# Infini-attention beside a gated MLP on one core: value projection of chunk 0 first, x copied by VectorE alone, first weights split over both load queues

## Chip, core and metric

One core of one Trainium2 chip. The metric is the device time of one execution in microseconds (us). Before the change it was 273.81 us (median of three runs, 273.72 to 274.2).

## The reference, cut to what matters

```python
def reference(A_x, A_wq, A_wk, A_wv, A_wo, A_beta, B_x, B_W_gate, B_W_up, B_W_down, gate_w):
    x = A_x                                   # [1, 2048, 512] bf16
    g = sigmoid((x * gate_w).sum(-1, keepdims=True))
    a = _A_ref(x, A_wq, A_wk, A_wv, A_wo, A_beta)     # 32 heads of 16, 4 segments of 512 tokens:
                                              # q, k, v = x @ wq, x @ wk, x @ wv; causal softmax within a
                                              # segment, mixed with a memory M, z carried over segments; @ wo
    b = _B_ref(x, B_W_gate, B_W_up, B_W_down) # relu(x @ W_gate) * (x @ W_up) @ W_down
    return g * a + (1 - g) * b
```

Segment (chunk) 0 has no memory yet. Its q, k and v projections are the first real work of the kernel.

## The kernel before

The kernel builds a list of operations for each engine. A list scheduler of its own then places them with a cost model and emits every engine's program in the order so found. A small change at the start can therefore change the order of everything that follows.

```python
    x0 = A_x[0, 0:512, :].rearrange("(i p) d -> p i d", p=128)
    for i, eng in enumerate(("sp", "act", "sp", "act")):
        load(eng, [f"hT{i}"], V.hT[:, i, :], x0[:, i, :], 1 << 17)
    for nm, w, src in (("wq", V.wq, A_wq), ("wk", V.wk, A_wk), ("wv", V.wv, A_wv)):
        for kt in range(KT):
            load("act" if nm == "wq" and kt % 2 else "sp", [f"{nm}{kt}"], w[:, kt, :], ...)
    # ... (cut)
    xps, xcs = [warm(5, 0, 3)], []            # 5 dummy matmuls on a zeroed tile
    for i in range(4):                        # transpose x: 4 matmuls against the identity per token tile
        # ... (cut) fx
        xps.append(pe(fx, 430, reads=[f"hT{i}", "ident"], writes=[f"bankL{i}"], name=f"xt{i}"))
        if i % 2 == 0:                        # PSUM -> xT, by turns on VectorE and ScalarE
            xcs.append(dve(... tensor_copy ..., name=f"xc{i}"))
        else:
            xcs.append(act(... activation Copy ..., name=f"xc{i}"))
    xps.append(warm(4, 1, 0))                 # 4 more dummies
    # ... (cut) inside proj(s): q and k tiles stream all 512 tokens of xT,
    #     v tiles use 128 tokens of xT as weights and stream wv
        if s == 0:
            pes = [p for k in "qkv" for p in pes if p.name[0] == k]      # all q, all k, all v
            pes[:2 * KT] = [pes[h * KT + kt] for kt in range(KT) for h in range(2)]
```

The scheduler's choice:

```python
    def _choose(self, e):                     # the next operation of engine e
        # the head of every queue of this engine, with the time at which the model thinks it is ready;
        # among those that are ready now, the one of the lowest priority number, then the earliest
```

The softmax here doesn't subtract the row's maximum and nothing guards it: scores larger than these inputs give would overflow.

## Time and profile before

| | before |
|---|---|
| time, median of three runs | 273.81 us |
| span in the profiled execution | 272.6 us |
| TensorE busy | 268.2 us (98%) |
| first q matmul | 6.74 us |
| end of the last matmul | 270.04 us |

The page's first part gives busy time per engine. TensorE is busy from the first microsecond to the last, so the rest of the reading asks which of its work is useful and what it waits for. In the lists of instructions the columns are start, length, engine, line, operation, result and operands, shape and count; the bracket gives the idle time before it and what ended that. In the tables of stretches each engine has its busy time and count, and the last three columns are the granted clock, the busy share of the DMA engines and GB/s. The lines themselves are in the prediction.

### The profile page before, as it was taken

The numbers are of one execution on the slowest core, as the hardware profiler recorded it, in microseconds if no ns is written. First come the engines' busy times: TensorE is split into PE (matmuls) and PEld (weight loads), VectorE is DVE, ScalarE is ACT, GpSimd is POOL, SyncE is SP. The second block draws the span as 40 slices with busy tenths as digits, with TensorE's granted clock in tenths as the row PEclk, the third lists the DMA queues.
The fourth block names the chain that finished last, engine by engine and source line by source line (L and its number), as shares of the span: only waits on it lengthen the run. The fifth ranks groups of instructions, "written<-read, shape, count | busy, mean of one in ns | idle before, by whom it ended". The sixth has DMA issues, their size and how long they took to land.

```text
span 272.6 us, 5368 instructions
## 1 busy us (share of the span) xinstructions
PE 268.2 (98%) x2156; PEld 115.6 (42%) x2156; DVE 206.0 (76%) x421; ACT 192.9 (71%) x182; POOL 123.2 (45%) x171
## 2 busy tenths in 40 slices
PE   7999999999999999999999999999999999999996
PEld 4444444344434544344344344344444343434445
DVE  5789989999989998999978949596774256787200
ACT  3279887788696877889578769985866768782122
POOL 4013566629495676847385653242233343331000
PEclk9999999999999999999999999999999999999999
DMA  6999964011001323120112110000111100000011
GB/s 203 332 333 172 290 97 90 13 42 39 20 2 40 79 58 79 38 53 9 22 39 60 38 48 32 19 2 0 25 35 22 38 23 19 0 2 1 0 41 38
DMA packets 31025, 17.01 MB, mean 62 GB/s; under 512 B 20760, under 2 KB 31000, under 8 KB 31000
## 3 DMA queue, kind: packets, MB, share of 16 engines
q1 hardware_dynamic: 30416, 16.14, 23.7%
q10 hardware_dynamic: 584, 0.53, 0.7%
q8 instruction: 17, 0.28, 0.4%
q14 instruction: 8, 0.07, 0.1%
HBM read 9.84 MB, written 2.10 MB: 44 GB/s over the span
## 4 chain that ended last, share of the span: by engine, by line
PE 94%; DVE 3%; DMA 1%; ACT 1%; issue 0%; DVEq 0%
PE psA L749 36%; PE psA L788 18%; PE psA L581 10%; PE psL L679 9%; PE psA L704 7%; PE psA L579 5%; PE psA L781 5%; DMA hT<-in_A_x_dram 1%; PE psA L654 1%; PE psA L625 1%; DVE gexpT L546 1%; PE psL L490 1%; ACT E L684 1%; PE psA L641 1%; DVE hT L760 1%; PE psL L482 0%
## 5 line engine op out<-in xcount | busy, mean ns | idle before, releaser
L684 ACT ACTIVATE E<-psL 128x2048 bf16<-128x2048 f32 x80 | 150.0, 1876 | 39.4 <-PE psL L679 38.8
L687 POOL TENSOR_SCALAR_AFFINE_SELECT E<-E 128x512 bf16<-128x512 bf16 x128 | 83.1, 667 | 116.1 <-ACT E L684 113.0
L749 PE MATMUL psA<-xT,wu 128*128 128x512 bf16 x224 | 59.8, 380 | 0.0
L749 PE MATMUL psA<-xT,wg 128*128 128x512 bf16 x224 | 59.5, 380 | 0.1
L788 PE MATMUL psA<-wd,hT 128*128 128x512 bf16 (+1 forms) x238 | 54.6, 367 | 0.0
L760 DVE TENSOR_TENSOR hT<-psA,rl 128x512 bf16<-128x512 f32 x56 | 38.2, 683 | 14.0 <-PE psA L749 13.1
L788 PEld LDWEIGHTS psA<-wd,hT 128*128 128x128 bf16 x238 | 21.7, 98 | 24.3 <-issue 3.7
L597 POOL TENSOR_SCALAR kp<-kT,pm 128x512 bf16<-128x512 bf16 x19 | 30.7, 1620 | 2.6 <-PE psL L679 1.2
L679 PE MATMUL psL<-qT,kp 32*128 32x384 bf16 (+3 forms) x512 | 31.7, 301 | 0.0
L749 PEld LDWEIGHTS psA<-xT,wu 128*128 128x128 bf16 x224 | 20.4, 98 | 25.4 <-issue 3.1
L749 PEld LDWEIGHTS psA<-xT,wg 128*128 128x128 bf16 x224 | 19.9, 98 | 24.7 <-issue 3.7
L709 DVE STREAM_TRANSPOSE Tn<-psA 128x512 f32<-128x512 f32 x32 | 21.5, 697 | 8.0 <-PE psA L704 7.9
L757 ACT ACTIVATE rl<-psA 128x512 bf16<-128x512 f32 x28 | 16.7, 597 | 12.7 <-PE psA L749 12.5
L679 PEld LDWEIGHTS psL<-qT,kp 32*128 32x128 bf16 x512 | 8.9, 92 | 31.7 <-ACT E L684 14.4
L758 DVE TENSOR_SCALAR rl<-psA 128x512 bf16<-128x512 f32 x28 | 19.0, 680 | 3.6 <-PE psA L749 2.9
L704 PE MATMUL psA<-E,vaug 128*17 128x256 bf16 (+3 forms) x512 | 21.1, 300 | 0.0
L581 PE MATMUL psA<-xT,wq 128*128 128x512 bf16 x64 | 16.5, 380 | 0.0
L781 PE MATMUL psA<-wo,oT 128*128 128x512 bf16 (+1 forms) x68 | 16.5, 367 | 0.0
L581 PE MATMUL psA<-xT,wk 128*128 128x512 bf16 x64 | 16.4, 381 | 0.0
L797 DVE TENSOR_SCALAR osb<-psA,omg 128x512 bf16<-128x512 f32 x8 | 6.0, 746 | 12.9 <-PE psA L788 12.9
L579 PE MATMUL psA<-wv,xT 128*128 128x512 bf16 x64 | 15.7, 380 | 0.0
L798 ACT ACTIVATE osb<-psA,omg 128x512 bf16<-128x512 f32 (+1 forms) x9 | 5.8, 639 | 13.7 <-PE psA L781 13.3
(75 smaller groups left out, 237.1 us busy)
## 6 DMA issues: line engine op xcount, KB each, us to landing
out_dram<-osb SPq DMA_DIRECT2D x15, 128.0 KB, 1.7
wg<-in_B_W_gate_dram SPq DMA_DIRECT2D x8, 224.0 KB, 5.3
wu<-in_B_W_up_dram SPq DMA_DIRECT2D x8, 224.0 KB, 5.8
wd<-in_B_W_down_dram SPq DMA_DIRECT2D x1, 1792.0 KB
osb<-in_A_x_dram SPq DMA_DIRECT2D x12, 128.0 KB, 2.2
wk<-in_A_wk_dram SPq DMA_DIRECT2D x4, 128.0 KB, 4.5
wv<-in_A_wv_dram SPq DMA_DIRECT2D x4, 128.0 KB, 4.0
wo<-in_A_wo_dram SPq DMA_DIRECT2D x1, 512.0 KB, 6.0
```

The lines of the kernel that those rows point to most:

```text
L579: ins = e.matmul(A(ep)[:, :], lhsT=V.xT[:, kt, tok + col * 128:tok + (col + 1) * 128], rhs=w[:, kt, :], start=(kt == 0), stop=(kt == KT - 1))
L581: ins = e.matmul(A(ep)[:, :], lhsT=w[:, kt, col * 128:(col + 1) * 128], rhs=V.xT[:, kt, tok:tok + 512], start=(kt == 0), stop=(kt == KT - 1))
L597: km = lambda e, G=G, p=p, ks=ks: e.tensor_scalar(V.kp[:, ks, :], V.kT[:, G, :], V.pm[:, p:p + 1], None, ALU.mult)
L679: ins = q.matmul(PL[:, jj, o:o + w], lhsT=V.kp[32 * jj:32 * jj + 32, kslot(s, n), 128 * j:128 * j + 128], rhs=V.qT[32 * jj:32 * jj + 32, q ...
L684: acts.append(act(lambda a, e=e: a.activation(V.E[:, e, :, :], PL[:, :, :], ACT.Exp, scale=SCALE), t_act(2048), reads=[f"bankL{b}" for b i ...
L687: pools.append(pool(lambda g, ap=ap: g.affine_select(out=ap, in_=ap, compare_op=ALU.is_ge, fill=0.0, base=0, pattern=[[0, 4], [1, 128]], c ...
L704: ins = q.matmul(A(ep)[32 * jj:32 * jj + 17, c:512], lhsT=V.vaug[:, s % 2, j, 8 * G + 2 * jj + p, :], rhs=V.E[:, e, jj, o:o + w], start=(j ...
L709: ds.append(dve(lambda e, p=p, ep=eps[p]: e.transpose(V.Tn[:, p, :], A(ep)[:, :]), t_dve(512), writes=[f"Tn{p}"], name=f"tr{s}_{G}_{p}", e ...
L749: ins = e.matmul(A(ep)[:, :], lhsT=w[:, kt, f * 128:(f + 1) * 128], rhs=V.xT[:, kt, c * 512:(c + 1) * 512], start=(kt == 0), stop=(kt == K ...
L760: evs.append(dve(lambda e, ep=eu, r=r, hs=hs: e.tensor_tensor(V.hT[:, hs, :], A(ep)[:, :], V.rl[:, r, :], ALU.mult), t_dve(512), reads=[f" ...
L781: ins = e.matmul(A(ep)[:, 0:c1 - c0], lhsT=V.oT[:, o0 + G, i * 128:(i + 1) * 128], rhs=V.wo[:, G, c0:c1], start=st_ and G == 0, stop=sp_ a ...
L788: ins = e.matmul(A(ep)[:, 0:c1 - c0], lhsT=V.hT[:, slots[f], i * 128:(i + 1) * 128], rhs=V.wd[:, f, c0:c1], start=st_ and f == f0, stop=sp ...
```

## The change

The intent is to replace the second block of dummies by work. A value tile needs one token tile of xT, so it may start after one of the four copies. To have wv in time, x comes over one queue and wv over the other, wq and wk follow on both, and the ScalarE queue issues them all before it loads its activation table. The x copies then all go to VectorE.

```diff
--- before.py
+++ after.py
@@ -413,12 +413,13 @@
     def load(eng, names, dst, src, nbytes, occ=460.0):
         (lact if eng == "act" else lsp).append(dma(eng, lambda e, dst=dst, src=src: e.dma_start(dst, src), nbytes, occ=occ, writes=names, name="ld" + names[0]))
     x0 = A_x[0, 0:512, :].rearrange("(i p) d -> p i d", p=128)
-    for i, eng in enumerate(("sp", "act", "sp", "act")):
-        load(eng, [f"hT{i}"], V.hT[:, i, :], x0[:, i, :], 1 << 17)
-    for nm, w, src in (("wq", V.wq, A_wq), ("wk", V.wk, A_wk), ("wv", V.wv, A_wv)):
+    for i in range(4):
+        load("sp", [f"hT{i}"], V.hT[:, i, :], x0[:, i, :], 1 << 17)
+        load("act", [f"wv{i}"], V.wv[:, i, :], A_wv[i * 128:(i + 1) * 128, :], 1 << 17)
+    for nm, w, src in (("wq", V.wq, A_wq), ("wk", V.wk, A_wk)):
         for kt in range(KT):
-            load("act" if nm == "wq" and kt % 2 else "sp", [f"{nm}{kt}"], w[:, kt, :], src[kt * 128:(kt + 1) * 128, :], 1 << 17)
-    load("act", ["g4"], V.g4[:], gate_w.rearrange("(kt p) -> kt p", p=128), 1 << 12)
+            load("act" if kt % 2 else "sp", [f"{nm}{kt}"], w[:, kt, :], src[kt * 128:(kt + 1) * 128, :], 1 << 17)
+    load("sp", ["g4"], V.g4[:], gate_w.rearrange("(kt p) -> kt p", p=128), 1 << 12)
     half = (NF // 2) * 128
     hs_ = ((0, half), (half, NF * 128))
 
@@ -470,7 +471,6 @@
     sc.queue(1, st)
 
     ds = []
-    ds.append(dve(lambda e: e.memset(V.rl[:, 0, 0:128], 0.0), 130, writes=["rl0"], name="warm0"))
     for b in range(4):
         ds.append(dve(lambda e, b=b: e.memset(PA[b][:], 0.0), 500, writes=[f"init{b}"], name=f"init{b}"))
     ds.append(dve(lambda e: e.reduce_sum(V.pm[:, :], pm8, AX.X), 180, reads=["pm8"], writes=["pm"], name="pm"))
@@ -479,11 +479,11 @@
     def warm(n, k, b):
         def fn(e):
             for i in range(n):
-                ins = e.matmul(PL[:, b, :], lhsT=V.rl[:, 0, 0:128], rhs=V.rl[:, 0, 0:128].unsqueeze(1).to_broadcast([128, 4, 128]), start=True, stop=True)
+                ins = e.matmul(PL[:, b, :], lhsT=nc.const_aps.tensor(1.0, [128, 128], BF16), rhs=nc.const_aps.tensor(1.0, [128, 512], BF16), start=True, stop=True)
             return ins
-        return pe(fn, n * (427 if k == 0 else 260), reads=["rl0"], writes=[f"bankL{b}"], name=f"warm{k}")
-
-    xps, xcs = [warm(5, 0, 3)], []
+        return pe(fn, n * 427, writes=[f"bankL{b}"], name=f"warm{k}")
+
+    xps, xcs = [warm(6, 0, 3)], []
     for i in range(4):
         def fx(e, i=i):
             for kt in range(KT):
@@ -492,14 +492,8 @@
         xps.append(pe(fx, 430, reads=[f"hT{i}", "ident"], writes=[f"bankL{i}"], name=f"xt{i}"))
         dst = V.xT[:, :, i * 128:(i + 1) * 128]
         srcp = PL[:, i, :].rearrange("q (k t) -> q k t", k=KT)
-        if i % 2 == 0:
-            xcs.append(dve(lambda e, d=dst, s_=srcp: e.tensor_copy(d, s_), t_dve(512), reads=[f"bankL{i}"], writes=[f"xT0_{i}"], name=f"xc{i}"))
-        else:
-            xcs.append(act(lambda e, d=dst, s_=srcp: e.activation(d, s_, ACT.Copy), t_act(512), reads=[f"bankL{i}"], writes=[f"xT0_{i}"], name=f"xc{i}"))
-    xps.append(warm(4, 1, 0))
-    sc.queue(0, xps)
-    sc.queue(0, [t for t in xcs if t.eng == "dve"])
-    sc.queue(0, [t for t in xcs if t.eng == "act"])
+        xcs.append(dve(lambda e, d=dst, s_=srcp: e.tensor_copy(d, s_), t_dve(512), reads=[f"bankL{i}"], writes=[f"xT0_{i}"], name=f"xc{i}"))
+    sc.queue(0, xcs)
 
     cst = [act(lambda e: e.activation(V.eb[:], V.braw[:], ACT.Exp), 300, reads=["braw"], writes=["eb"], name="eb")]
     cst.append(dve(lambda e: e.tensor_scalar(V.romgh[:], V.eb[:], 1.0, None, ALU.add), 190, reads=["eb"], writes=["romgh"], name="romgh"))
@@ -571,7 +565,7 @@
         def pj(w, col, name, wname, tokmajor=False):
             ep = Epoch("proj")
 
-            step = 1 if s == 0 and name == "q" and col < 2 else 2
+            step = 2
             for k0 in range(0, KT, step):
                 def fn(e, k0=k0):
                     for kt in range(k0, k0 + step):
@@ -580,7 +574,7 @@
                         else:
                             ins = e.matmul(A(ep)[:, :], lhsT=w[:, kt, col * 128:(col + 1) * 128], rhs=V.xT[:, kt, tok:tok + 512], start=(kt == 0), stop=(kt == KT - 1))
                     return ins
-                pes.append(pe(fn, mm(512, step), reads=[f"{wname}{kt}" for kt in range(k0, k0 + step)] + xt(s), name=f"{name}{s}_{col}", ep=ep, role="w2" if k0 else "w"))
+                pes.append(pe(fn, mm(512, step), reads=[f"{wname}{kt}" for kt in range(k0, k0 + step)] + ([f"xT0_{col}"] if s == 0 and tokmajor else xt(s)), name=f"{name}{s}_{col}", ep=ep, role="w2" if k0 else "w"))
             return ep
         for G in range(4):
             ep = pj(V.wq, G, "q", "wq")
@@ -606,8 +600,9 @@
             ep = pj(V.wv, tt, "v", "wv", True)
             evs.append(dve(lambda e, ep=ep, tt=tt: e.tensor_copy(V.vaug[:, s % 2, tt, :, 0:16], A(ep)[:, :].rearrange("q (h c) -> q h c", c=16)), t_dve(512), writes=[f"va{s % 2}_{tt}"], name=f"vcp{s}_{tt}", ep=ep, role="r"))
         if s == 0:
-            pes = [p for k in "qkv" for p in pes if p.name[0] == k]
-            pes[:2 * KT] = [pes[h * KT + kt] for kt in range(KT) for h in range(2)]
+            vs = [p for p in pes if p.name[0] == "v"]
+            pes = [p for p in pes if p.name[0] != "v"]
+            sc.queue(0, xps[:3] + vs[0:1] + xps[3:4] + vs[1:2] + xps[4:] + vs[2:])
         return pes, evs, sbs, acts, sps
 
     def va(s):
```

## The prediction

> **What bounds the kernel now.** I read the page's busy shares and chain first, then the waits of TensorE, then TensorE's instructions in order of time, then the groups of the tile xT, the stretches of the first 8 us, and the landing times of single loads.
>
> The page of the kernel before, busy time and chain:
> ```profile
> PE 268.2 (98%) x2156; PEld 115.6 (42%) x2156; DVE 206.0 (76%) x421; ACT 192.9 (71%) x182; POOL 123.2 (45%) x171
> ...
> PE 94%; DVE 3%; DMA 1%; ACT 1%; issue 0%; DVEq 0%
> ```
> TensorE is busy for 268.2 of 272.6 us and is 94% of the chain that ends last. Busy could still hide waits, so I look at what TensorE waited for in the whole run:
> ```profile
> PE psL L482 <- DVE rl L473: 1.0, 1, 1.0
> PE psL L490 <- DMA hT<-in_A_x_dram: 0.4, 1, 0.4
> PE psA L641 <- DVE phiq L592: 0.2, 1, 0.2
> ```
> Two of the three waits are before the first transposition; the third is 0.2 us at 85 us. So from the first projection on there is nothing to win but TensorE's own work, and this change does not touch that work. What it can win is in the opening. TensorE's first instructions in order of time (start, length, line, result, operands, count):
> ```profile
> 1.04 2.32 PE L482 MATMUL psL<-rl 128*128 128x512 bf16 x5 [1.04 <-DVE rl L473]
> 3.79 1.89 PE L490 MATMUL psL<-ident,hT 128*128 128x128 bf16 x16 [0.44 <-DMA hT<-in_A_x_dram]
> 5.48 1.43 PE L482 MATMUL psL<-rl 128*128 128x512 bf16 x4
> 6.74 1.89 PE L581 MATMUL psA<-xT,wq 128*128 128x512 bf16 x8
> ```
> L482 is a warm-up on a dummy tile. Five of them fill the wait for x, four more fill 5.48 to 6.74, while xT is copied out of PSUM. They count as busy and as chain, but give no result. The 1.26 us of the second block are what the change goes after: work is to be done there that has to be done anyway.
>
> Why the first projection cannot start earlier is in the groups of the tile xT:
> ```profile
> L496 DVE CAST xT<-psL x2: 691/692/693, 4.4 to 5.3; 128x512 bf16<-128x512 f32 x2
> L498 ACT ACTIVATE xT<-psL x2: 597/597/597, 4.9 to 5.7; 128x512 bf16<-128x512 f32 x2
> ```
> The last copy starts at 5.72 and takes 0.60, so it ends at 6.32, and every q matmul streams all four token tiles. A value matmul takes one token tile of xT as its weights, so it needs one copy only. That is the idea of the change.
>
> **What the Trainium skill says.** "TensorE: Matmul & The Clock Gate", Part 1, says that TensorE starts at 1.2 GHz and goes to 2.4 GHz after a busy window of about 3.4 us, and that this window runs freely. The trace agrees on the speeds: the warm-ups at 1.04 follow each other every 427 ns, the L581 matmuls at 6.74 every 216 ns, and the one that starts at 5.90 needs 404 ns. So the clock rises at about 6.3 us. The 16 transpositions, every 107 ns, are slow too. "DMA: Bandwidth & Descriptors", Issuing engines are not separate DMA queues, says that both load queues share the same 16 engines, and that two issuers save only issue time. The trace agrees (stretches, GB/s last):
> ```profile
> 3.00:3.70 0.70, 0.35 (x1) 0.00 (x0) 0.25 (x2) 0.43 (x1) 0.56 (x3) 1.00 1.07 356
> 3.70:4.20 0.50, 0.41 (x5) 0.41 (x6) 0.00 (x0) 0.50 (x1) 0.50 (x2) 1.00 0.94 145
> 4.20:4.70 0.50, 0.50 (x7) 0.50 (x6) 0.26 (x1) 0.35 (x1) 0.27 (x1) 1.00 0.90 176
> 4.70:5.20 0.50, 0.50 (x8) 0.50 (x6) 0.43 (x1) 0.33 (x1) 0.00 (x0) 1.00 0.65 225
> 5.20:6.20 1.00, 1.00 (x7) 0.58 (x6) 0.69 (x1) 0.74 (x2) 0.00 (x0) 1.00 1.08 374
> ```
> About 370 GB/s is the ceiling here, so one 128 KB tile takes 0.35 us and a pair (one on each queue) 0.70, though a queue issues one every 0.45. And there is a **dip** from 3.7 to 5.2. "ScalarE: Activation LUTs", What ACT_TABLE_LOAD costs, gives 1283 ns for the load; the trace has 1.28 us (3.27 to 4.55), partly inside the dip. The page says the load copies from slots in the engine, not over the DMA, so I don't take it as the dip's cause.
>
> **The change part by part.**
> (1) Loads. Today x goes two and two on the queues; the first pair, issued at 0.78, lands 2.8 and 3.0 us later (3.6 and 3.75), the second 2.9 and 3.1 after its issue (4.15 and 4.35). The third pair is wq, issued at 1.7: 4.5 and 4.7, so 6.2 and 6.4, and the next at 6.9 and 7.2. After the change SP brings x0 to x3 and ACT wv0 to wv3. So x0 still comes at 3.75 and x1 at 4.35, but x2 and wv2 are now the third pair and x3 and wv3 the fourth. Everything hangs on whether the dip hits them. Without it: third pair 4.35 + 0.70 = 5.05, fourth 5.75. With it, as today: 6.4 and 7.2.
> (2) Warm-up: six dummies on a constant, no wait for the DVE memset. They start at about 0.85 and end at 0.85 + 6 x 0.427 = 3.4, as now. The four later ones are gone.
> (3) Copies: all four of xT on DVE at 0.69, instead of two there and two on ACT at 0.60. They are now spread over time, one per transposition. ACT may load its table at 4.4 instead of 3.27 (eight issues of 0.45 from 0.78) without anyone waiting, as its first real work is the key exponentials at 12 us.
> (4) TensorE's order (from the two programs built side by side): transpositions 0 and 1; v tile 0, contraction tiles 0 and 1; transposition 2; v tile 0, tiles 2 and 3; transposition 3; v tiles 1 to 3; then q and k groups by turns. By hand, without the dip: transposition 0 from 3.79 to 4.21; 1 from 4.41 to 4.84; copy 0 from 4.44 to 5.13, so v tile 0 begins at 5.2 and does two slow matmuls to 6.05; transposition 2 to 6.4; v tile 0 ends at 6.8; transposition 3, now fast, 7.0; v tiles 1 to 3, 12 x 0.216 = 2.6, end at 9.6. All copies are in time for these. With the dip: transposition 2 waits for 6.4 and ends at 6.7, wv3 comes at 6.9, v tile 0 ends at 7.4, transposition 3 at 7.65, v at 10.25.
> Compare at the same amount of work: today q starts at 6.74, and the 16 value matmuls are worth 16 x 0.216 = 3.46, so the break-even is 10.20. The gain of the opening is **0.6 us without the dip and 0 with it**.
> (5) The rest is placed anew by the kernel's own list scheduler, so all later instructions shift. Counted from both programs, the number of matmuls of every kind is the same but for three dummies fewer. Changes of array shape: entries of the E-by-value groups between full matmuls fall by one (5 to 4, and 18 to 17 out). In and out each cost about 0.1 us over a plain matmul (309 instead of 216 ns in; 152 instead of 46 out): 0.2 us gained. The last part of the order is the same in both. Today's stalls after 6.74 sum to about 0.6 us (two of 0.28 at 85 and 129 us, some small ones); the new order will have others, I take 0.6 plus or minus 0.3.
> Sum: without the dip 0.6 + 0.2 = 0.8, so 273.81 - 0.8 = 273.0; with it 273.6.
>
> **The rivals.**
> (a) The dip moves with the third pair (a limit of the queues, or of time). For it: it sits exactly at today's third pair. Against: it comes when the engines first read wq, a new tensor, and a similar first read would now come after the fourth pair. Then 273.6.
> (b) TensorE's order is in place, so a late wv3 blocks transposition 3, and the new idle pieces (0.2 + 0.35, or 1.2 with the dip) thin out the window in which the clock is judged. If the rise comes one window of 3.4 us later, the last 12 value matmuls run at 427 instead of 216 ns: 2.5 us lost, 275.6 to 276.1. Against: today there is already 0.43 us idle in that window, and it rose.
> (c) ACT or DVE become the bound, because the attention starts later. Against: the first exponential starts at 14.46 today; in the new order five groups of 0.87 come ahead of it from 9.6, so 14.0. DVE is at 76%, and the two copies it takes over are 1.4 us in an idle stretch. Worth 0.
> (d) A bad gap in the reordered middle: some tenths either way.
>
> **Range and chances.** I give the case without the dip 0.5 (273.0), the dip 0.35 (273.6), the late clock 0.1 (275.8), something else 0.05. The middle of this is 273.2. The low end is the case in which the clock rises early and the shapes help as well: another 0.8 us below 273.0, 272.2. The high end, 274.7, leaves out most of the late clock. 2% is 5.5 us; the whole opening before the first projection is 6.74 us and most of it is the wait for x, so faster by 2% is as good as out of reach: 0.01. Slower by 2% needs the late clock and bad gaps together: 0.02.
>
> **What would show it.** Right: value matmuls from about 5.2; q from about 9.6 and no later than 10.2; x2 landing near 5.05 and x3 near 5.75; no wait over 0.4 us in the opening but that for x0; DVE and ACT nowhere named in TensorE's waits after it; the end of TensorE 0.6 to 0.8 us earlier. Wrong: x2 or wv3 landing after 6.4 (the dip moved), value matmuls every 427 ns after 6.5 us (late clock), or new waits of TensorE in the middle that sum to over 1 us.

## The result

The changed kernel took **276.37 us** (median of four runs, 275.45 to 276.71), the kernel before 273.76 (273.36 to 274.2, four runs). The ratio is 1.0089, with a 95% interval of 1.0061 to 1.0118. Ratios here are the mean time of one kernel's fast runs over that of the other's in the same rounds, so not quite the ratio of the medians that are quoted. The change cost 2.6 us by the medians. It lies outside the predicted range (272.2 to 274.7) and has the wrong sign.

The page of the changed kernel, busy time and chain:

```profile
PE 264.9 (96%) x2117; PEld 115.2 (42%) x2153; DVE 206.8 (75%) x413; ACT 196.1 (71%) x194; POOL 116.5 (42%) x166
...
PE 90%; DVE 3%; issue 2%; DMA 2%; ACT 2%; ACTq 0%; DVEq 0%
```

The 3.3 us less of TensorE's busy time are not to be taken at their word: 36 of its matmul records are missing from this trace (2117 matmuls against 2153 weight loads). A missing record shows as a 0.2 us wait ended by "issue", so those waits are not read. Its place in the chain fell from 94% to 90%. The opening of TensorE, in order of time:

```profile
0.82 2.72 PE L482 MATMUL psL<-const-bfloat16-1.0 128*128 128x512 bf16 x6 [0.82 <-PEq L876]
3.46 1.20 PE L490 MATMUL psL<-ident,hT 128*128 128x128 bf16 x8
4.94 1.01 PE L573 MATMUL psA<-wv,xT 128*128 128x512 bf16 x2 [0.28 <-DVE xT L495]
5.78 0.61 PE L490 MATMUL psL<-ident,hT 128*128 128x128 bf16 x4
6.76 1.01 PE L573 MATMUL psA<-wv,xT 128*128 128x512 bf16 x2 [0.37 <-DMA wv<-in_A_wv_dram]
7.57 0.63 PE L490 MATMUL psL<-ident,hT 128*128 128x128 bf16 x4
7.99 3.69 PE L573 MATMUL psA<-wv,xT 128*128 128x512 bf16 x12
11.52 1.03 PE L575 MATMUL psA<-xT,wq 128*128 128x512 bf16 x4
```

Here is the first finding. The value matmuls at 4.94 and 6.76 take 1.01 us for two. The twelve at 7.99 take 3.69 us; at full speed they take 2.75. The last slow one starts at 9.27, and the next one, at 9.70, lasts 310 ns to its successor: the clock rises at about 9.9 us and not at 6.3. The first q matmul starts at 11.52. The profile's row of the granted clock shows full speed throughout; this slow start isn't in it and is read from the spacing of matmuls (427 or 216 ns at 512 columns). The packed trace does keep the moment of the rise in some runs; see e3_again below.

What TensorE waited for in the whole run after its first instruction, the named waits that sum to 0.3 us or more:

```profile
PE psA L649 <- DVE Tn L704: 0.6, 1, 0.6
PE psA L573 <- DMA wv<-in_A_wv_dram: 0.4, 1, 0.4
PE psL L674 <- ACT E L679: 0.3, 2, 0.2
PE psA L573 <- DVE xT L495: 0.3, 1, 0.3
```

The waits of L573 belong to the opening. The other two lines are new, in the middle of the kernel (125.4, 128.1 and 130.5 us), and they are the second finding. Around the longest (VectorE and TensorE, in order of time):

```profile
123.36 1.24 DVE L540 COPY gexpT<-gexp 32x4 f32<-32x4 f32 x4
...
124.63 1.31 DVE L704 STREAM_TRANSPOSE Tn<-psA 128x512 f32<-128x512 f32 x2
...
125.40 0.41 PE L649 MATMUL psA<-Mbd,phiq 128*128 128x128 bf16 x4 [0.59 <-DVE Tn L704]
```

VectorE copies four little gate tiles for 1.24 us, and only then transposes the two value accumulators out of PSUM. TensorE wants one of these banks for the next memory group and stands still for 0.59 us.

The two findings add up. Let q's start be compared at equal work: the value tiles are worth 16 x 0.216 = 3.46 us, so 6.74 + 3.46 = 10.20 is the break-even. From 10.20 to the end of the last matmul the kernel before takes 259.84 us. The changed one starts q at 11.52 and ends at 272.08.

| | before | changed | difference |
|---|---|---|---|
| q starts, at equal work | 10.20 | 11.52 | **+1.32** |
| from there to the last matmul's end | 259.84 | 260.56 | **+0.72** |
| sum, profiled runs | | | +2.04 |

The profiled run of before was one of its slower ones (274.32); this is why the medians differ by 2.6 and not by 2.04. So 10.20 is the break-even of that one launch: the same opening began q at 6.11 us in e8_before_newrest and at 7.08 in e7_before_fillrest.

### The profile page after: what moved, and what is told of

Read it like the earlier page. It is cut to its first block, busy times and chain, and to the rows that moved or that the text cites. A ratio compares the mean times of both kernels' runs of the same rounds, so it can differ in the third digit from the quotient of the medians.

```text
span 274.6 us, 5331 instructions
## 1 busy us (share of the span) xinstructions
PE 264.9 (96%) x2117; PEld 115.2 (42%) x2153; DVE 206.8 (75%) x413; ACT 196.1 (71%) x194; POOL 116.5 (42%) x166
## 3 DMA queue, kind: packets, MB, share of 16 engines
q10 hardware_dynamic: 1152, 1.05, 1.2%
## 4 chain that ended last, share of the span: by engine, by line
PE 90%; DVE 3%; issue 2%; DMA 2%; ACT 2%; ACTq 0%; DVEq 0%
PE psA L744 34%; PE psA L783 17%; PE psA L575 10%; PE psL L674 9%; PE psA L699 7%; PE psA L573 5%; PE psA L776 5%; DMA wv<-in_A_wv_dram 2%; ACT E L679 1%; PE psA L620 1%; PE psA L649 1%; DVE gexpT L540 1%; DVE Tn L704 1%; PE psA L636 1%; DVE hT L755 1%
## 5 line engine op out<-in xcount | busy, mean ns | idle before, releaser
L744 PE MATMUL psA<-xT,wg 128*128 128x512 bf16 x212 | 57.6, 380 | 1.7 <-issue 1.6
L744 PE MATMUL psA<-xT,wu 128*128 128x512 bf16 x219 | 58.3, 380 | 0.5 <-issue 0.3
L783 PE MATMUL psA<-wd,hT 128*128 128x512 bf16 (+1 forms) x230 | 53.1, 367 | 1.0 <-issue 0.8
L755 DVE TENSOR_TENSOR hT<-psA,rl 128x512 bf16<-128x512 f32 x56 | 38.2, 684 | 11.1 <-PE psA L744 10.4
L752 ACT ACTIVATE rl<-psA 128x512 bf16<-128x512 f32 x30 | 17.9, 596 | 11.6 <-PE psA L744 11.0
L591 POOL TENSOR_SCALAR kp<-kT,pm 128x512 bf16<-128x512 bf16 x14 | 22.6, 1611 | 1.7 <-DVE rdg L709 1.1
L753 DVE TENSOR_SCALAR rl<-psA 128x512 bf16<-128x512 f32 x26 | 17.7, 682 | 2.6 <-PE psA L744 1.9
L793 ACT ACTIVATE osb<-psA,omg 128x512 bf16<-128x512 f32 (+1 forms) x12 | 7.8, 652 | 15.5 <-PE psA L776 13.3
L573 PE MATMUL psA<-wv,xT 128*128 128x512 bf16 x62 | 17.0, 412 | 0.9 <-DMA wv<-in_A_wv_dram 0.4
L575 PE MATMUL psA<-xT,wq 128*128 128x512 bf16 x60 | 15.6, 379 | 0.5 <-issue 0.5
L699 PEld LDWEIGHTS psA<-E,vaug 128*17 128x17 bf16 x512 | 10.6, 90 | 10.9 <-issue 2.8
```

The source lines that it names most:

```text
L573: ins = e.matmul(A(ep)[:, :], lhsT=V.xT[:, kt, tok + col * 128:tok + (col + 1) * 128], rhs=w[:, kt, :], start=(kt == 0), stop=(kt == KT - 1))
L575: ins = e.matmul(A(ep)[:, :], lhsT=w[:, kt, col * 128:(col + 1) * 128], rhs=V.xT[:, kt, tok:tok + 512], start=(kt == 0), stop=(kt == KT - 1))
L591: km = lambda e, G=G, p=p, ks=ks: e.tensor_scalar(V.kp[:, ks, :], V.kT[:, G, :], V.pm[:, p:p + 1], None, ALU.mult)
L699: ins = q.matmul(A(ep)[32 * jj:32 * jj + 17, c:512], lhsT=V.vaug[:, s % 2, j, 8 * G + 2 * jj + p, :], rhs=V.E[:, e, jj, o:o + w], start=(j ...
L744: ins = e.matmul(A(ep)[:, :], lhsT=w[:, kt, f * 128:(f + 1) * 128], rhs=V.xT[:, kt, c * 512:(c + 1) * 512], start=(kt == 0), stop=(kt == K ...
L755: evs.append(dve(lambda e, ep=eu, r=r, hs=hs: e.tensor_tensor(V.hT[:, hs, :], A(ep)[:, :], V.rl[:, r, :], ALU.mult), t_dve(512), reads=[f" ...
```

## The experiments

Theory: (1) TensorE's idle pieces between 3.3 and 6.8 us (0.12 + 0.19 + 0.49 + 0.58 = 1.38 us, against one piece of 0.65 in the kernel before) make the clock rise one window later; (2) the newly placed rest costs 0.7 us by itself. Rivals: the launch alone sets the moment of the rise; everything was lost in the opening; the loads are to blame. The window is the one of 3.4 us that the prediction names with its source. The idle pieces are the spacing of two starts less the 427 or 107 ns of a slow matmul; the brackets of the profile, whose ends are modelled, say less (0.44 for the 0.65).

To try one thing at a time I had the scheduler run twice on paper inside the build, once for the kernel itself and once for a reference kernel, and then forced an order: what the reference starts before its first gate matmul of the MLP (the opening) in the kernel's own order, all that follows in the reference's order, on every engine.

```diff
     def _choose(self, e):
+        if self.forced is not None:           # next not yet placed operation of the given order
+            ...
```

### Two dummies in the gap: e1_fill

```diff
-            sc.queue(0, xps[:3] + vs[0:1] + xps[3:4] + ...)
+            sc.queue(0, xps[:3] + [warm(2, 5, 3)] + vs[0:1] + xps[3:4] + ...)   # the rest is placed anew
```

> The changed kernel with two dummy matmuls put between transposition 1 and value tile 0, so that TensorE has hardly an idle piece from 3.4 to 6.7 us; the list scheduler places the rest anew. Theory (the idle pieces in the opening made the clock rise one window later, at 10.0 us instead of 6.3): the clock rises before 7 us, value tiles 1 to 3 run every 216 ns, q starts near 10.0 us instead of 11.5, the time falls by about 1.5 us to 274.9 (the newly placed rest may add or take 0.5). Rival (the moment of the rise is set by the launch and not by what TensorE does between 3 and 7 us): the rise stays at 10 us and the time at 276.4 or above.

Measured: 273.14 us (272.77 to 273.6), ratio to before 0.9965 (0.9945 to 0.9985). In the trace the clock rises near 4.6 us and q starts at 9.64:

```profile
7.05 2.75 PE L670 MATMUL psA<-wv,xT 128*128 128x512 bf16 x12
9.64 1.03 PE L672 MATMUL psA<-xT,wq 128*128 128x512 bf16 x4
```

That is better than expected by 1.8 us, and the trace shows why: the rest, placed anew, takes 259.07 us and has no named wait after 14 us at all.

### The old order of the rest, without and with the dummies: e3_oldrest, e4_fill_oldrest

The edit of e3_oldrest is the forced order alone, with the kernel before as the reference; e4_fill_oldrest has the two dummies as well.

> The changed kernel's opening (loads, dummies, value tiles first, copies on DVE), and after it every instruction in the order of the kernel before. Theory (the newly placed rest costs about 0.7 us in stalls between 80 and 130 us, besides the late clock): the clock still rises near 10 us, the time falls from 276.4 to 275.7. Rival (everything lost was lost in the opening): 276.4, within 0.2.

> Both: two dummies in the opening and the old order of the rest. Theory: both losses go, 276.4 - 1.5 - 0.7 = 274.2, with q starting near 10.0 against the break-even of 10.2, so about level with the kernel before (273.8). Rival (launch sets the rise): no better than e3_oldrest.

Measured: e3_oldrest 275.96 us (273.82 to 276.83), e4_fill_oldrest 274.37 us (274.23 to 274.48), ratio to before 1.0008 (0.9989 to 1.0028). The rest takes 259.94 and 259.93 us, as in the kernel before. With the dummies q starts at 10.18, at the break-even. So with an early clock and the old order of the rest the change is worth nothing that these runs can tell. One run of e3_oldrest was at 273.82 while its others were at 275.82, 276.1 and 276.83.

### The same kernel again: e3_again

> The changed kernel's opening with the old order of the rest a second time, for the share of launches with a late clock. In e3_oldrest and in the changed kernel 7 of 8 launches were at 275.4 or above and one at 273.8; with the two dummies (e1_fill, e4_fill_oldrest) none of 8. Theory: at least half of the launches are above 275.3 and the others near 274.2, hardly any between, since the phase of the window alone decides. Rival (a steady loss in the opening): all within 0.5 of one value.

Measured: 274.4, 274.51, 274.55, 275.37, 275.66 and 276.3 us. Three of six were early, three up to 1.9 us late, though two of these lie between the extremes, so "hardly any between" did not hold. The profiled launch was an early one this time. TensorE's lines of value tiles 1 to 3 and of the first q, e3_oldrest (275.82 us in this execution):

```profile
8.24 3.53 PE L670 MATMUL psA<-wv,xT 128*128 128x512 bf16 x12
11.60 1.03 PE L672 MATMUL psA<-xT,wq 128*128 128x512 bf16 x4
```

and e3_again (274.40 us), the same program:

```profile
7.59 2.75 PE L678 MATMUL psA<-wv,xT 128*128 128x512 bf16 x12
10.18 1.03 PE L680 MATMUL psA<-xT,wq 128*128 128x512 bf16 x4
```

One program, two launches: the twelve value matmuls take 3.53 or 2.75 us, q starts at 11.60 or 10.18, and the times differ by just these 1.42 us. This is the cost of the late clock, measured without any change of code: 0.78 us of it in the twelve, 0.58 in the slow matmuls of value tile 0 and transposition 3 just before them, 0.06 in a later load. It also shows that the launch has a say. Does the program have one too? Over all runs with this opening and no filler (the changed kernel, e3_oldrest and e3_again), 9 of 14 were about 1 us or more above the early value (274.4 for the old rest; 275.0 for the new one, whose rest is 0.62 longer). With the two dummies (e1_fill, e4_fill_oldrest, e1_again) it was 0 of 14. These counts go by time, as most runs have no trace, and the cut is not sharp: 275.37 is 0.97 above its early value and counted, 274.19 of e1_again is 0.93 above its profiled run and not. At 1.0 us the counts are 8 and 0, at 0.9 us 9 and 1. The reading that fits is that the launch decides where the window lies, and the idle pieces decide in how many launches it fails.

The record backs this in two places.

First, the packed traces (trace.npz, which `prof` does not print in full) of nine runs keep the moment at which the full clock was granted, and it agrees with the spacing of the matmuls: 6.27 us before, 9.88 in the changed kernel, 9.80 in e3_oldrest, 4.57 in e1_fill, 4.90 in e4_fill_oldrest. The stretches at full clock that follow last 266.24 us in seven traces and 269.65 in two, which is 78 and 79 times 3.413 us. This fits a clock that changes only at the ends of windows of that length. I estimated from the starts of the matmuls how long TensorE was idle in such windows. The window that ended with the rise held 0.0 to 0.65 us of it in these nine traces, and 0.87 (e5_bigloads) and 0.91 (e3_again, rise near 5.5 us) where the rise is read from spacing; the window before it, which failed, held 1.05 (e3_oldrest), 1.12 (changed kernel), 1.2 (e9_nodummies) and 1.84 (e6_delay; the rise of e9_nodummies is again read from spacing, near 10.4 us). Only e7_before_fillrest, with 0.85 in a window that failed, overlaps. So nearly the same pieces passed in e3_again, where the last of them came after the rise, and failed in e3_oldrest, whose window took in most of them.

Second, the four of the 14 that lie furthest above their early value (276.71 of the changed kernel, 276.1 and 276.83 of e3_oldrest, 276.3 of e3_again; 1.7 to 2.4 us above it) list a mean granted clock of 0.994, every other run 0.999 or more. That is 0.6% of 275 us, or about 3.3 us at half the clock (an estimate): one more window. No trace of these four was kept, so what happened in them stays open.

### Dummies taken from the kernel before: e2_nowarm2, e9_nodummies

```diff
-    xps.append(warm(4, 1, 0))                 # e2: the second block; e9: the first block as well
```

Every other instruction keeps its order.

> The kernel before without its second block of four dummies, every other instruction in the same order on every engine, so that TensorE idles from 5.7 to about 6.4 us. Theory (idle pieces delay the clock): the rise comes near 9.7 us, q matmuls run every 427 ns until then, about half of 3.3 us is lost, 275.3. Rival (launch sets the rise): the rise stays at 6.3, q starts up to 0.3 us earlier, 273.5.

> The kernel before without either block of dummies, all other instructions in the same order. TensorE's first work is then transposition 0 at 3.75 us. Theory (the clock rises at the end of a freely running window of 3.4 us in which TensorE idled little; idle of about 0.65 us in the window still passed, 1.3 us failed): no window that ends before about 6.9 us can pass, so the rise comes between about 6.9 and 10.3 us in every launch, q runs slow from 6.4 on, the time rises by 0.3 to 1.9 us, mean about 275.0, more spread than before. Rival (dummies don't matter): 273.7 to 274.0.

Measured: e2_nowarm2 274.0 us (273.65, 273.8, 274.2 and 275.36), ratio 1.0005 (0.9974 to 1.0035): my expectation of 275.3 missed. In its trace the clock rose between the last transposition (5.1) and the first q matmul (6.19), by the packed trace at 5.39. The gap had only begun then, so this launch doesn't test it. One of four runs is 1.4 us up. e9_nodummies: 276.17 us (275.27 to 276.79), ratio 1.0074 (1.0051 to 1.0096), late in every run, and by more than I had expected. In its trace (transpositions, then the first eight q matmuls):

```profile
3.87 1.89 PE L585 MATMUL psL<-ident,hT 128*128 128x128 bf16 x16 [3.87 <-DMA hT<-in_A_x_dram]
6.45 3.60 PE L680 MATMUL psA<-xT,wq 128*128 128x512 bf16 x8 [0.69 <-ACT xT L593]
```

Eight q matmuls take 3.60 us instead of 1.89. With the second block gone, the first is thus worth 2.2 us; the second alone hardly anything in most launches.

### The order of the rest alone: e8_before_newrest, e7_before_fillrest

The opening is that of the kernel before; the order of the rest is that of the changed kernel (e8) or of e1_fill (e7).

> The opening of the kernel before, and after it the order of the changed kernel. Its clock rises early, so the placement of the rest stands alone. Theory: 0.7 us more than the kernel before, 274.7. Rival (the rest costs nothing by itself, it only looked so beside a late clock): 274.0, within 0.2.

> The opening of the kernel before (loads, dummies, q first), and after it every instruction in the order that the list scheduler gave to e1_fill. Theory (from q's break-even to TensorE's last matmul the rest took 259.07 us in e1_fill, 259.85 in the kernel before, 260.56 in the changed kernel, so the 0.9 us by which e1_fill beats the kernel before is a better placed rest and not value tiles going first): 0.8 us less than the kernel before, 273.2. Rival (the gain is the new opening): level with the kernel before, 274.0.

Measured: e8_before_newrest 274.66 us (274.38 to 274.87), ratio 1.0019 (1.0002 to 1.0036). Its clock rose at 5.2 us, and the 0.59 us wait for VectorE's transposition is there again, at 123.6 us:

```profile
PE psA L752 <- DVE Tn L807: 0.6, 1, 0.6
```

The new order costs about 0.5 to 0.6 us by itself by the times, 0.9 by this one trace (from 9.57, the break-even with q at 6.11, to 270.32 are 260.75 us against 259.84). e7_before_fillrest gave 274.12 us (273.22 to 274.37), ratio 0.9989 (0.9963 to 1.0015), so the expected 0.8 us did not show in the time. In its trace no named wait is left after 14 us, but the clock rose only at about 7.6 us and q began at 7.08, which ate the gain in that launch. I count this one as inconclusive; the better pair is e4_fill_oldrest against e1_fill, whose rests take 259.93 and 259.07 us on the same opening.

### What slows the loads: e6_delay, e5_bigloads

In the kernel before and in the changed one the loads run slow from about 3.7 to 5 us. The changed kernel (stretches; last column GB/s):

```profile
3.00:3.70 0.70, 0.70 (x5) 0.25 (x4) 0.14 (x2) 0.00 (x0) 0.56 (x3) 1.00 1.00 342
3.70:4.20 0.50, 0.50 (x6) 0.25 (x4) 0.10 (x1) 0.00 (x0) 0.50 (x2) 1.00 0.82 189
4.20:4.70 0.50, 0.46 (x4) 0.19 (x2) 0.50 (x1) 0.08 (x1) 0.27 (x1) 1.00 0.94 248
4.70:5.20 0.50, 0.26 (x1) 0.14 (x2) 0.50 (x2) 0.50 (x1) 0.00 (x0) 1.00 0.89 283
```

Its third pair of loads is x2 and wv2, which landed at 5.7 and 5.9 us, and wv3 at 6.6. Both runs are on the kernel before: e6_delay holds the first load of each queue back by a wait; e5_bigloads loads x and wq in pieces of 256 KB.

```diff
-    for i, eng in enumerate(("sp", "act", "sp", "act")):
-        load(eng, [f"hT{i}"], V.hT[:, i, :], x0[:, i, :], 1 << 17)
+    for i, eng in ((0, "sp"), (2, "act")):     # e5; wq likewise
+        load(eng, [f"hT{i}", f"hT{i + 1}"], V.hT[:, i:i + 2, :], x0[:, i:i + 2, :], 1 << 18)
```

> The kernel before with the first load of each queue held back by a wait for the second PSUM memset of VectorE, about 1.3 us, all orders kept. If the slow stretch belongs to the loads (the third pair, or after 0.5 MB), it moves along to about 4.9 to 6.4 us and x0 to x3 land at 4.9 to 5.7. If it belongs to the moment, it stays at 3.6 to 5.0 and falls on the first pairs, which land late, and no slow stretch follows 5.2. The time rises by about 1.3 us and perhaps a late clock; it is not what is asked.

> The kernel before with x and wq in one load of 256 KB per queue each instead of two of 128 KB, all orders kept. It asks what makes the loads slow from 3.6 to 5 us. If the third load of a queue is what is slow, x and wq are now loads one and two and wq lands by 5.3 us, and q starts at 6.4 instead of 6.74: 273.7. If it is the amount (after 0.5 MB) or the moment, wq lands at 6.2 to 7.2 as before, and q that needs both halves starts at about 7.0 or later: 274.0 to 274.5.

The stretches of e6_delay, one run (276.05 us, state unknown):

```profile
4.20:4.90 0.70, 0.00 (x0) 0.00 (x0) 0.00 (x0) 0.25 (x1) 0.27 (x1) 1.00 1.10 379
4.90:5.40 0.50, 0.41 (x5) 0.41 (x6) 0.00 (x0) 0.50 (x1) 0.00 (x0) 1.00 1.09 305
5.40:5.90 0.50, 0.50 (x7) 0.50 (x6) 0.27 (x1) 0.50 (x1) 0.00 (x0) 1.00 0.76 254
5.90:6.40 0.50, 0.50 (x8) 0.50 (x6) 0.43 (x1) 0.37 (x2) 0.00 (x0) 1.00 1.02 342
```

The slow stretch moved along with the loads, so it isn't the moment, though it is milder here. The stretches of e5_bigloads:

```profile
3.70:4.20 0.50, 0.19 (x2) 0.19 (x3) 0.00 (x0) 0.08 (x1) 0.50 (x2) 1.00 1.09 383
4.20:4.70 0.50, 0.50 (x7) 0.50 (x6) 0.04 (x1) 0.00 (x0) 0.28 (x1) 1.00 1.10 377
4.70:5.20 0.50, 0.50 (x8) 0.50 (x6) 0.50 (x1) 0.12 (x1) 0.00 (x0) 1.00 1.04 336
```

There is none after the first 0.5 MB: x and wq landed 3.2, 3.5, 4.1 and 4.5 us after their issue, wq at 5.4 and 5.8 us instead of 6.2 to 7.2. So neither the moment nor the amount fits, and of the three candidates the third load of a queue is left. But e5_bigloads changed the size of the loads as well as their number, and its own third load on SP shows no slow stretch (354 and 359 GB/s from 5.4 to 6.4 us). The third load fits only if it starts late after its issue and the 1 MB ahead of it hides that: issued at 1.81 us, it landed at 6.19, and the third of the kernel before, issued at 1.73, at 6.41. That loads of 128 KB are slow at the start as such is a rival that no run here excludes. The time of e5_bigloads, however, was 274.9 us (274.28 to 275.48), not 273.7. Its profiled launch began q at 6.45 as expected and was the fastest (274.28). The slower launches have no trace. x0 now lands later, TensorE idles for 0.86 us instead of 0.65 before the first transposition, and a later clock in some launches would fit; this is argued and not shown.

### A version from this: e1_again, e10_vbig

e10_vbig is e1_fill with x in two loads of 256 KB on SP and wv in two on ScalarE's queue, and seven first dummies instead of six; the order is that of e1_fill.

> e1_fill a second time, unchanged, to see whether it beats the kernel before on another day and by how much. Theory: 0.3 to 0.9 us below the kernel before, no launch with a late clock, so all within 0.6 us of each other. Rival (the first result was luck of the phase): level with the kernel before, or launches 1.5 us up.

> e1_fill with x in two loads of 256 KB on SP and wv in two on ACT (each queue's third load, the slow one, is then wq, which is not needed before 9 us), seven dummies first, all orders kept. Theory (the slow third load took away the gain of the changed opening): x2, x3, wv2 and wv3 land by 5.9 us instead of 5.6 to 6.4, q starts at about 9.45 instead of 9.64, up to 0.3 us below e1_again. Against it: x0 lands at 4.0 instead of 3.4 to 3.75, which eats part of it. Rival (the loads are not what bounds this opening): level with e1_again within 0.1.

Measured, on one chip: e1_again 273.53 us (273.24 to 274.19), ratio 0.9984 (0.9967 to 1.0001), so not clear of level, and spread over 0.95 us instead of the 0.6 expected; **e10_vbig 273.09 us** (272.81 to 273.52), ratio 0.9965 (0.995 to 0.998). TensorE in e10_vbig (transpositions 0 and 1, value tiles 1 to 3, first q):

```profile
4.26 0.62 PE L585 MATMUL psL<-ident,hT 128*128 128x128 bf16 x8 [0.34 <-DMA hT<-in_A_x_dram]
...
6.84 2.75 PE L678 MATMUL psA<-wv,xT 128*128 128x512 bf16 x12
9.43 1.03 PE L680 MATMUL psA<-xT,wq 128*128 128x512 bf16 x4
```

q starts at 9.43 as expected, against 9.88 in e1_again, and the rest takes the same 259.07 us. So this version beats both kernels: 0.9 us below the kernel before, 3.3 below the changed one, which ran in other rounds. Of the 0.9 us, 10.20 - 9.43 = 0.77 is the opening and 259.84 - 259.07 = 0.77 the order of the rest by the traces; the profiled runs differ by 1.51 (274.32 and 272.81), the medians by less, since before's was one of its slower runs and this one of the faster. Whether it was the larger loads or the seventh dummy that gave the last 0.4 us was not separated. The traces speak for the loads: the second half of value tile 0 starts at 6.18 us here, and at 6.64 in e1_again, after a wait of 0.40 us for wv. But the clock also rose earlier in this launch, before 4.26 us against about 4.5, which made both transpositions fast.

## Why the prediction was wrong

- **The step that failed is the choice between the cases of the opening.** I named the mechanism as rival (b): idle pieces thin out the window and the rise comes 3.4 us later, 275.6 to 276.1. I gave it 0.1, because "today there is already 0.43 us idle in that window, and it rose". The same opening was late in 9 of 14 runs. One launch that had passed with one short gap (0.43 by the profile's ends, 0.65 by spacing) said nothing about an opening with four gaps and 1.38 us, and not how near to failing it had been. The prediction had the warning itself: it worked out 1.2 us of new idle for the case with the dip, gave that case 0.35, and yet kept the late clock at 0.1.
- **Its size** was put at 2.5 us for twelve slow matmuls. Measured within one program it was 1.42 us: the clock rose at 9.8 us, in the middle of the twelve (at 9.9 in the changed kernel). That the 275.6 to 276.1 of rival (b) came near the measured 276.37 is in part luck: the late clock cost less than that, and the new order made up for it.
- **Step (5) was mis-sized.** I took the stalls of the rest as unchanged "plus or minus 0.3" and credited 0.2 us for fewer changes of shape. The new order cost 0.72 us in the traces of the two kernels, 0.5 to 0.6 alone by the times of e8_before_newrest, by waits of TensorE for VectorE's and ScalarE's release of PSUM. Another placement had none of them. The spread between three placements is 1.5 us (259.07 to 260.56), so the term had to carry 0.8 us either way.
- **The slow stretch of the loads did hit the third pair.** My odds for it (0.35 against 0.5) are not refuted by one outcome, but the argument against it, the first read of a new tensor, is: in the changed kernel the first new tensor, wv, is in the first pair. With an early clock the gain of the opening came out as in my second case: q at 10.18, nothing won.
- **Two sums of the range.** The chances give a mean of 273.5, not 273.2, and the "another 0.8 us" of the low end counts again the 0.6 and 0.2 that were already in the 273.0. Neither would have saved the range.
- **Right:** TensorE's work sets the end; the first value matmul at about 5 us (4.94); no bound on ScalarE or VectorE as a whole; the identical tail; nothing near 2% to be won.

## What to carry to other kernels

In the opening of this kernel, dummy matmuls were worth more than early real work with gaps. Fill the gaps before the clock has risen, and look at the spread over launches, not at one trace. When a list scheduler places the rest, a change of the opening draws a new order for everything; hold the rest fixed before you judge the opening, and try several orders, since they differ by as much as the change itself. Where several loads are needed at once at the start, try few large ones per queue: here wq landed earlier in e5_bigloads, and x3 and wv3 in e10_vbig, but x0 came later in both, and e5_bigloads was slower than the kernel before for a reason that was not shown.

## What the Trainium skill lacked or had wrong

- "TensorE: Matmul & The Clock Gate", Part 1, puts the rise about 4 us into sustained activity, plus or minus 0.5 us by the window's phase. Here, with TensorE at work from 0.8 to 1.0 us on, it came anywhere from just before 4.3 to 7.6 us in launches of openings with dummies that were not late, at 9.8 and 9.9 us in late ones, and the same program did both (275.82 and 274.40 us). The same Part reports 6, 11 or 14 slow matmuls for one kernel, which is nearer to this spread. It warns of idle gaps of more than about 3 us once warm; before the rise, pieces of 0.1 to 0.6 us were enough to make 9 of 14 runs late, and two dummies brought that to 0 of 14 (by time, with the cut described under e3_again). How much idle a window tolerates is not given; by the estimate above it lay near 0.9 us here, and these runs don't settle it more closely.
- The same page advises not to fit the cold start, since it is under 1% of a typical span. It is 0.5% here (1.42 us), and for work on a tuned kernel that is the whole effect.
- "DMA: Bandwidth & Descriptors" has nothing on a slow stretch after a queue's first two loads: with 128 KB per load the rate fell from 356 to between 145 and 225 GB/s for 1.5 us after two loads per queue (kernel before), and with 256 KB per load it stayed at 336 to 383 GB/s over the same stretch.
- The first page warns that a trace's clock events can be unreliable. No page says that the profile's view of the granted clock stays at 1.00 before the first recorded rise, while matmuls of 512 columns follow each other every 427 ns; the slow start has to be read from their spacing, or from the moment of the rise, which nine of the fourteen packed traces keep.
